# Three slices of the first expert layer's weights on chip, their loads moved, its units taken in threes

## The chip, the cores and the metric

One NeuronCore of a Trainium2 chip runs the whole program; the other cores idle. The metric is the device time of one launch in microseconds (us), as the median of several runs. TensorE (PE) multiplies matrices, VectorE (DVE), ScalarE (ACT) and GpSimd (POOL) work elementwise, SyncE (SP) only issues transfers; each engine takes its instructions strictly in its own order. ACT issues transfers too.

## The reference

Three stages, on 4 batches of 576 tokens (2304 rows of 512 after attention).

```
a = softmax of phi over the sequence;  k_m = a.T @ k;  v_m = a.T @ v      # 32 memory slots a head
x = softmax(q @ k_m.T / 8) @ v_m                                          # 8 heads of 64, joined to 512
h = x @ w_in;  x = (h * cos(h)) @ w_out                                   # w_in 512x2048, w_out 2048x512
out = sum over 4 experts e of p[:, e] * (relu(x @ w1[e]) @ w2[e])         # p = domain_probs, rows scaled to sum 1
```

## The kernel before

**Numbers.** A float32 operand of a large product is split into a rounded high part and the rest, both of type fp32r, and a product is three matmuls (`mm3`, L145): high by high, high by low, low by high. `w_in` and `w_out` arrive as 64-bit floats: `narrow` (L122) loads a chunk of 512 KB into one of two buffers `raw64`, ACT rescales it (L131), and DVE shifts and merges the halves in three passes (L132, L133, L136) into 32-bit floats. `split_w` (L106) then makes the two parts of a `w_out` slice, with ACT (L109) and four pieces on POOL, or two on POOL and two on DVE for slices after the second (L111).

**Attention** is a generator (L167) of 8 parts, two groups of four heads for each batch. A part loads phi, then k, v and q; takes a maximum (DVE L189), an exponential (ACT L207) and a sum (L209) over the sequence; projects k and v on the 32 slots (PE L221); and makes scores (PE L271), which DVE transposes (L278) and reduces (L281), POOL subtracts (L282), ACT exponentiates (L285), DVE sums and inverts (L286 to L288), POOL scales (L289) and DVE transposes back (L293); ACT and POOL split the result into `attnT` (L103, L104). k and v share three buffers `kv`, phi and q have two each.

**The first expert layer** is cut into 8 slices of 256 hidden columns. A unit is a slice and a batch: `project` (L316) folds v into the slice of `w_in` (PE, 16 records of `vw_ps`); `hidden1` (L333) makes h on PE (24 matmuls of `hp`) and h times cosine on ACT, DVE (L360, L365, L104) and POOL; `output1` (L369) multiplies with `w_out` (48 matmuls of `op`), and DVE adds the results into `acc` (L384 for slice 0, L386 after it). While attention still runs, units are in a narrow form (one chunk of 128 hidden columns at a time, POOL subtracts, DVE makes the low part of `gt`); afterwards in a wide form (L354), which takes both chunks in one instruction.

**Order of the units.** `order` (L391) runs slices 0 and 1 over all batches first (8 units), and then slices 2 to 7, each over the four batches. Buffers: `wi` and `wo` two each, `wf` one. Slice 0's `w_in` is issued by SP ahead of the loads of batch 1, and its `w_out` and all of slice 1 by ACT, each behind one of the first exponentials (`exps`). Six units stand among the attention parts 2 to 7, one to a part, each behind its part's scores (L438 to L441); the seventh and later ones are wide. Slice 2 is loaded from units 6 and 8 on, and later slices during the slice ahead of them (L402).

**What sets the order.** The program is traced in the order of the code, and a scheduler then lays it out engine by engine along a time line of its own, so that an instruction may move far from its place in the code. SP's queue is strictly in order too: a transfer that waits for a buffer holds up those behind it.

**The second expert layer** (L459 on) follows; its code is the same in both kernels. The sums of `domain_probs` that it needs (`load_probs`, L92) are loaded by POOL near the start: 2304 pieces of 16 bytes.

Of the kernel before, what the change touches and what calls it, by code (L numbers as in the profile page):

```python
# [9 lines left out]
F32 = mybir.dt.float32  # L10
F32R = mybir.dt.float32r
# [13 lines left out]
def tile_kernel(  # L25
# [13 lines left out]
    nc = tc.nc  # L39
    B, H, S, D = q.shape  # L40
    M = phi.shape[3]
    NT, DM = out.shape
# [6 lines left out]
    KD = DM // 128  # L49
    FS = 256  # L50
    NFC = FS // 128
    NS1 = DFF // FS
# [37 lines left out]
    p_all = const.tile([128, NT // 128, E], F32, name="p_all")  # L90

    def load_probs():  # L92
        nc.gpsimd.dma_start(out=p_all, in_=probs.rearrange("(i p) e -> p i e", p=128))
        p_sum = const.tile([128, NT // 128], F32, name="p_sum")
        nc.vector.tensor_reduce(out=p_sum, in_=p_all, axis=AX.X, op=ALU.add)
        nc.vector.tensor_scalar_add(p_sum, p_sum, 1e-9)
        nc.vector.reciprocal(out=p_sum, in_=p_sum)
        nc.vector.tensor_tensor(
            out=p_all, in0=p_all, in1=p_sum[:, :, None].to_broadcast([128, NT // 128, E]), op=ALU.mult
        )  # L100

    def split(hi, lo, src, eng=None):
        nc.scalar.activation(out=hi, in_=src, func=ACTF.Copy)  # L103
        (eng or nc.vector).tensor_tensor(out=lo, in0=src, in1=f32(hi), op=ALU.subtract)  # L104

    def split_w(t, src, early=False):  # L106
        t, src = t.rearrange("p x a b -> p x (a b)"), src.rearrange("p a b -> p (a b)")
        n = src.shape[1]
        nc.scalar.activation(out=t[:, 0], in_=src, func=ACTF.Copy)  # L109
        for c in range(0, n, 256):  # L110
            (nc.vector if early and c % 512 else nc.gpsimd).tensor_tensor(  # L111
                out=t[:, 1, c:c + 256], in0=src[:, c:c + 256], in1=f32(t[:, 0, c:c + 256]), op=ALU.subtract
            )
# [8 lines left out]
    def narrow(w, src, after=None, part=None):  # L122
        n, m = w.shape[1:]
        c = 1024 // (2 * m)
        for i in range(0, n, c) if part is None else (part * c,):
            raw = cw.tile([128, c, 2 * m], U32, tag="raw64", name="raw64")
            with tc.issue_after(after.ins) if after else nullcontext():
                (nc.scalar if after else nc.sync).dma_start(out=raw, in_=src[:, i:i + c])
            lo, hi = (raw.rearrange("p a (b t) -> p a b t", t=2)[:, :, :, t] for t in range(2))
            hif = raw.bitcast(F32).rearrange("p a (b t) -> p a b t", t=2)[:, :, :, 1]  # L130
            nc.scalar.activation(out=hif, in_=hif, func=ACTF.Copy, scale=2.0 ** -112)  # L131
            nc.vector.tensor_single_scalar(lo, lo, 29, op=ALU.logical_shift_right)  # L132
            nc.vector.scalar_tensor_tensor(  # L133
                out=lo, in0=hi, scalar=3, in1=lo, op0=ALU.logical_shift_left, op1=ALU.bitwise_or
            )
            nc.vector.scalar_tensor_tensor(  # L136
                out=w[:, i:i + c].bitcast(U32),
                in0=hi,
                scalar=0x80000000,
                in1=lo,  # L140
                op0=ALU.bitwise_and,
                op1=ALU.bitwise_or,
            )
# [13 lines left out]
    cw = cs_ctx.enter_context(tc.tile_pool(name="cw", bufs=2))  # L157
    mb = cs_ctx.enter_context(tc.tile_pool(name="mb", bufs=1))
    cs = cs_ctx.enter_context(tc.tile_pool(name="cs", bufs=2))
# [5 lines left out]
    exps = []  # L165
# [133 lines left out]
    wi = {}  # L299
    wo = {}  # L300
    wf = [None]

    def load_in(s, after=None, part=None):
        if not part:
            wi[s] = cw.tile([128, KD, FS], F32, tag="wi", name="wi")
        narrow(wi[s], w_in_v[:, :, 2 * s * FS:2 * (s + 1) * FS], after, part)

    def load_out(s, after=None, part=None):
        if not part:
            wf[0] = cw.tile([128, NFC, DM], F32, tag="wf", name="wf", bufs=1)  # L310
        narrow(wf[0], w_out_v[:, s * NFC:(s + 1) * NFC, :], after, part)
        if part != 0:
            wo[s] = cs.tile([128, 2, NFC, DM], F32R, tag="wo", name="wo")
            split_w(wo[s], wf[0], s > 1)

    def project(b, wi):  # L316
        vw_ps = ps_o.tile([128, 2, FS], F32, tag="o", name="vw_ps")
        for g in range(2):
            for i in range(HG):
                nc.tensor.matmul(  # L320
                    out=vw_ps[32 * i:32 * i + 32, g, :],
                    lhsT=vz[b][:, g, i, :],
                    rhs=wi[:, 2 * g + i // 2, :],
                    start=True,
                    stop=True,
                )
        vw = cs.tile([128, 2, 2, FS], F32R, tag="vw", name="vw")
        split(vw[:, 0], vw[:, 1], vw_ps)
        return vw
# [39 lines left out]
    def output1(s, b, th, gt, wo):  # L369
        for d in range(KD):  # L370
            c = d % 2 if wide[0] else 0
            op = (ps_o, ps_a)[c].tile([128, 512], F32, tag="oa"[c], name="op")
            for fc in range(NFC):
                mm3(
                    op[:, :TH],
                    lambda x: wo[:, x, fc, d * 128:d * 128 + 128],
                    lambda x: gt[:, x, fc, :],
                    fc == 0,
                    fc == NFC - 1,
                )  # L380
            t0 = (b % 2) * S
            dst = x1v[:, b // 2, d, t0:t0 + S].rearrange("p (c u) -> p u c", u=2)[:, th]
            if s == 0:
                nc.vector.tensor_copy(out=dst, in_=op[:, :TH])  # L384
            else:
                nc.vector.tensor_tensor(out=dst, in0=op[:, :TH], in1=dst, op=ALU.add)  # L386
# [1 line left out]
    vws = {}  # L388
    wide = [False]
    pend = []  # L390
    order = [(s, b) for b in range(B) for s in range(2)]  # L391
    order += [(s, b) for s in range(2, NS1) for b in range(B)]

    def project_next(n):
        if n + 1 < len(order):
            s2, b2 = order[n + 1]
            vws[n + 1] = project(b2, wi[s2])

    def step1(n):
        s, b = order[n]  # L400
        for th in range(2):
            if n > 8 and b in (1, 2) and s + 1 < NS1:  # L402
                (load_in, load_out)[b - 1](s + 1, marks[-1], th)
            pend.append((s, b, th, hidden1(b, th, vws[n]), wo[s]))
            if len(pend) > 2:
                output1(*pend.pop(0))
            if th == 0:
                project_next(n)

    parts = [attention(b, g) for b in range(B) for g in range(2)]  # L410
# [3 lines left out]
    def warm_up(n):  # L414
        for _ in range(n):
            nc.tensor.matmul(out=warm, lhsT=ones, rhs=ones, start=True, stop=True)

    for i in (0, 1, 0, 1, 0, 1, 0, 0, 1, 1):
        next(parts[i], None)
    warm_up(25)  # L420
    load_in(0)
    load_out(0, exps[0])
    vws[0] = project(0, wi[0])
    for i in (2, 2, 3, 2, 3):
        next(parts[i])
    load_in(1, exps[0])
    load_out(1, exps[1])
    nu = 0
    for n in range(2, np_):
        part = parts[n]  # L430
        if n + 2 < np_:
            next(parts[n + 2])
        if n + 1 < np_:
            next(parts[n + 1])
        if n + 2 < np_:
            next(parts[n + 2])
        next(part)
        next(part, None)  # L438
        if n <= 7:
            step1(nu)  # L440
            nu += 1  # L441
    wide[0] = True
    c_ctx.close()
    ps_h[0] = p_ctx.enter_context(tc.tile_pool(name="ps_h2", bufs=2, space=PSUM, reuse_waits="tile"))
    load_probs()
    at_ctx.close()
    wc = ctx.enter_context(tc.tile_pool(name="wc", bufs=2, side="right", reuse_waits="tile"))
    for n in range(nu, len(order)):
        s, b = order[n]
        if n == 6:  # L450
            load_in(2)
        if n == 8:
            load_out(2)
        step1(n)
    for p in pend:
        output1(*p)
# [216 lines left out]
```

## Time and profile before

| | |
|---|---|
| median of 3 runs | 1220.98 us (1220.67 to 1222.85) |
| profiled execution | 1223.36 us, its span 1221.6 us |
| PE busy | 1181.9 us, 97% of the span |
| DVE, ACT, POOL busy | 868.2, 485.6, 525.2 us |
| moved by transfers | 72.89 MB |

The page splits the span into 40 slices of 30.5 us and gives in each the busy share of every engine, the clock granted to TensorE and the transfers. PE is short of full in the first five slices alone. Attention fills about the first 160 us; from there to 440 us the first expert layer runs alone, and then the second to the end.

### The profile page before, as it was taken

What the parts mean: (1) busy time and instruction counts of PE and PEld (TensorE: products, weight loads), DVE (VectorE), ACT (ScalarE), POOL (GpSimd) and SP (SyncE); (2) the same over time, 40 slices, a digit from 0 to 9 for tenths busy, and PEclk for the clock granted to TensorE, in tenths of its full rate; (3) what the DMA queues carried; (4) which work ended last, traced back from release to release, by engine and by line L of the source; (5) the groups of instructions that cost most, each with busy time, mean ns of one, the idle gap of its engine ahead of it and who ended that gap; (6) DMA issues with size and microseconds to landing.
All of it is one profiled execution on the core that took longest, in us unless ns stands there. A gap on an engine that the chain in (4) does not pass through costs nothing.

```text
span 1221.6 us, 20025 instructions
## 1 busy us (share of the span) xinstructions
PE 1181.9 (97%) x7946; PEld 1050.3 (86%) x7946; DVE 868.2 (71%) x1571; ACT 485.6 (40%) x854; POOL 525.2 (43%) x609
## 2 busy tenths in 40 slices
PE   6788999999999999999999999999999999999998
PEld 5466788999999988888889898898889989888997
DVE  5798988798788788666666666678656665666665
ACT  2475755666566663232222223244222322322221
POOL 1443533332333852445445445546534544453420
PEclk8589999999999999999999999999999999999999
DMA  9953001112112110111111111113111111111102
GB/s 224 251 147 77 21 36 52 36 53 70 35 36 72 52 52 18 37 52 51 35 53 53 35 40 57 43 36 129 54 35 50 55 35 35 53 52 36 52 1 78
DMA packets 48062, 72.89 MB, mean 60 GB/s; under 512 B 2624, under 2 KB 31328, under 8 KB 47968
## 3 DMA queue, kind: packets, MB, share of 16 engines
q1 hardware_dynamic: 41024, 55.85, 16.1%
q10 hardware_dynamic: 6880, 15.73, 4.2%
q8 instruction: 62, 1.02, 0.3%
q14 instruction: 32, 0.26, 0.1%
q0 software_dynamic: 64, 0.04, 0.0%
HBM read 66.88 MB, written 4.72 MB: 59 GB/s over the span
## 4 chain that ended last, share of the span: by engine, by line
PE 62%; DVE 1%; issue 0%
PE op L147 33%; PE hp L147 29%; DVE x L485 1%; DVE sA L477 0%; DVE sB L498 0%; DVE acc L617 0%; DVE ht L582 0%; DVE u L558 0%; DVE acc L386 0%
## 5 line engine op out<-in xcount | busy, mean ns | idle before, releaser
L147 PE MATMUL op<-wb,ht 128*128 128x512 f32 x1728 | 439.3, 396 | 0.0
L147 PEld LDWEIGHTS hp<-x,wa 128*128 128x128 f32 x2688 | 380.3, 189 | 24.4 <-DVE x L485 3.6
L147 PE MATMUL hp<-x,wa 128*128 128x320 f32 (+1 forms) x2688 | 393.6, 295 | 3.2 <-DVE x L485 2.9
L147 PEld LDWEIGHTS op<-wb,ht 128*128 128x128 f32 x1728 | 312.7, 188 | 58.5
L617 DVE SCALAR_TENSOR_TENSOR acc<-op,p_all,acc 128x512 f32<-128x512 f32 x270 | 201.8, 748 | 137.7 <-PE op L147 137.4
L147 PE MATMUL op<-gt,wo 128*128 128x288 f32 x1536 | 228.8, 298 | 6.3 <-DVE acc L384 3.2
L147 PEld LDWEIGHTS op<-gt,wo 128*128 128x128 f32 x1536 | 211.7, 189 | 13.1 <-DVE acc L384 4.0
L111 POOL TENSOR_TENSOR wb<-raw,wb 128x256 fp32r<-128x256 f32 x124 | 89.5, 753 | 227.2 <-ACT wb L109 227.2
L588 ACT ACTIVATE ht<-c 128x256 fp32r<-128x256 f32 (+3 forms) x128 | 71.8, 562 | 283.5 <-DVE c L558 283.5
L104 POOL TENSOR_TENSOR gt<-y,gt 128x576 fp32r<-128x576 f32 x52 | 81.4, 1566 | 163.2 <-ACT gt L103 138.5
L589 DVE SCALAR_TENSOR_TENSOR ht<-c,ht 128x256 fp32r<-128x256 f32 (+3 forms) x128 | 93.7, 732 | 63.1 <-ACT ht L588 63.1
L147 PE MATMUL hp<-attnT,vw 128*128 128x288 f32 x768 | 129.6, 304 | 4.9 <-DVE y L365 3.8
L528 POOL TENSOR_TENSOR wa<-raw,wa 128x256 fp32r<-128x256 f32 x96 | 69.2, 748 | 149.1 <-ACT wa L518 149.1
L147 PEld LDWEIGHTS hp<-attnT,vw 128*128 128x128 f32 x768 | 109.6, 190 | 19.1 <-issue 14.3
L558 DVE TENSOR_TENSOR c<-hp,u 128x256 f32<-128x256 f32 (+1 forms) x192 | 87.3, 457 | 42.3 <-PE hp L147 37.9
L528 POOL TENSOR_TENSOR wa<-tt,wa 128x256 fp32r<-128x256 f32 x128 | 110.0, 889 | 0.0
L386 DVE TENSOR_TENSOR acc<-op,acc 128x288 f32<-128x288 f32 x224 | 96.5, 450 | 16.5 <-PE op L147 16.1
L565 ACT COPY p<-hp 128x256 f32<-128x256 f32 x64 | 25.7, 401 | 113.0 <-PE hp L147 113.0
L364 ACT ACTIVATE y<-y 128x576 f32<-128x576 f32 (+1 forms) x76 | 46.1, 609 | 61.3 <-DVE y L356 52.9
L103 ACT ACTIVATE gt<-y 128x576 fp32r<-128x576 f32 (+1 forms) x76 | 46.0, 605 | 37.6 <-DVE y L365 37.5
L518 ACT ACTIVATE wa<-raw 128x512 fp32r<-128x512 f32 x32 | 20.2, 632 | 85.5 <-PE hp L147 85.3
L365 DVE TENSOR_TENSOR y<-hp,y 128x576 f32<-128x576 f32 (+1 forms) x76 | 49.7, 655 | 5.2 <-ACT y L364 5.0
(101 smaller groups left out, 1062.4 us busy)
## 6 DMA issues: line engine op xcount, KB each, us to landing
raw<-in_moe_w_dram SPq DMA_DIRECT2D x60, 512.0 KB, 3.5
raw<-in_moe_w_out_dram ACTq DMA_DIRECT2D x14, 512.0 KB, 3.5
raw<-in_moe_w_in_dram ACTq DMA_DIRECT2D x12, 512.0 KB, 3.7
kv<-in_k_dram SPq DMA_DIRECT2D x16, 288.0 KB, 6.2
kv<-in_v_dram SPq DMA_DIRECT2D x16, 288.0 KB, 7.1
q<-in_q_dram SPq DMA_DIRECT2D x8, 576.0 KB, 9.2
out_dram<-acc SPq DMA_DIRECT2D x18, 256.0 KB, 2.0
phi<-in_phi_dram SPq DMA_DIRECT2D x8, 288.0 KB, 7.9
```

What stands on the lines that cost most here:

```text
L103: nc.scalar.activation(out=hi, in_=src, func=ACTF.Copy)
L104: (eng or nc.vector).tensor_tensor(out=lo, in0=src, in1=f32(hi), op=ALU.subtract)
L111: (nc.vector if early and c % 512 else nc.gpsimd).tensor_tensor(out=t[:, 1, c:c + 256], in0=src[:, c:c + 256], in1=f32(t[:, 0, c:c + 256]) ...
L147: nc.tensor.matmul(out=ps, lhsT=lt(a), rhs=rt(b), start=first and i == 0, stop=last and i == 2, skip_group_check=more,)
L364: nc.scalar.activation(out=y, in_=y, func=ACTF.Sin, scale=-TWO_PI if wide[0] else TWO_PI)
L365: nc.vector.tensor_tensor(out=y, in0=hv, in1=y, op=ALU.mult)
L386: nc.vector.tensor_tensor(out=dst, in0=op[:, :TH], in1=dst, op=ALU.add)
L528: pool.tensor_tensor(out=wa[:, 1, o], in0=src, in1=f32(wa[:, 0, o]), op=ALU.subtract)
L558: nc.vector.tensor_tensor(out=out, in0=ps[:, :n], in1=sb, op=ALU.add)
L588: nc.scalar.activation(out=ht[:, 0, fc, lo:], in_=c[:, fc, lo:], func=ACTF.Relu)
L589: nc.vector.scalar_tensor_tensor(out=ht[:, 1, fc, lo:], in0=c[:, fc, lo:], scalar=0.0, in1=f32(ht[:, 0, fc, lo:]), op0=ALU.max, op1=ALU.su ...
L617: nc.vector.scalar_tensor_tensor(out=dst, in0=op, scalar=pe, in1=dst, op0=ALU.mult, op1=ALU.add)
```

## The change

Three slices are on chip at first instead of two (`bufs=3` for `wi` and `wo`), and the order of units becomes slices 0, 1 and 2 over all batches (12 units), then 3 to 7. All weight loads at the start are issued by SP: slice 0 right behind the loads of batch 0, slice 1's `w_in` ahead of the second pair of attention parts and its `w_out` behind their loads, slice 2 at part 2. The first unit is traced ahead of part 2's scores, and after that one unit follows an even part and two an odd one, so that nine narrow units are traced among the parts instead of six. `domain_probs` is loaded by SP. The memory kept for POOL's own transfers is cut to 2048 bytes.

```diff
-        nc.gpsimd.dma_start(out=p_all, in_=probs.rearrange("(i p) e -> p i e", p=128))
+        nc.sync.dma_start(out=p_all, in_=probs.rearrange("(i p) e -> p i e", p=128))
...
-            wi[s] = cw.tile([128, KD, FS], F32, tag="wi", name="wi")
+            wi[s] = cw.tile([128, KD, FS], F32, tag="wi", name="wi", bufs=3)
...
-            wo[s] = cs.tile([128, 2, NFC, DM], F32R, tag="wo", name="wo")
+            wo[s] = cs.tile([128, 2, NFC, DM], F32R, tag="wo", name="wo", bufs=3)
...
-    order = [(s, b) for b in range(B) for s in range(2)]
-    order += [(s, b) for s in range(2, NS1) for b in range(B)]
+    NE = 3
+    order = [(s, b) for b in range(B) for s in range(NE)]
+    order += [(s, b) for s in range(NE, NS1) for b in range(B)]
...
-            if n > 8 and b in (1, 2) and s + 1 < NS1:
+            if n >= NE * B and b in (1, 2) and s + 1 < NS1:
...
-    for i in (0, 1, 0, 1, 0, 1, 0, 0, 1, 1):
+    for i in (0, 1, 0, 1):
+        next(parts[i], None)
+    load_in(0)
+    load_out(0)
+    for i in (0, 1, 0, 0, 1, 1):
         next(parts[i], None)
     warm_up(25)
-    load_in(0)
-    load_out(0, exps[0])
     vws[0] = project(0, wi[0])
+    load_in(1)
     for i in (2, 2, 3, 2, 3):
         next(parts[i])
-    load_in(1, exps[0])
-    load_out(1, exps[1])
+    load_out(1)
...
+        if n == 2:
+            step1(nu)
+            nu += 1
+            load_in(2)
+            load_out(2)
         next(part)
         next(part, None)
-        if n <= 7:
+        for _ in range(n % 2 if n == 2 else 1 + n % 2):
             step1(nu)
             nu += 1
...
-        if n == 6:
-            load_in(2)
-        if n == 8:
-            load_out(2)
+        if n == NE * B - 3:
+            load_in(NE)
+        if n == NE * B - 1:
+            load_out(NE)
...
-    nc = _bacc.Bacc("TRN2", target_bir_lowering=False, num_devices=1)
+    nc = _bacc.Bacc("TRN2", target_bir_lowering=False, num_devices=1, dynamic_dma_scratch_size=2048)
```

The queue of SP before, from the second half of slice 0's `w_in` on (`kv_128` is the last of the k and v of part 1, `kv_426` the first of part 2):

```order
L128 DMA raw64_387<-in_moe_w_in_dram 128x2x512
L171 DMA phi_424<-in_phi_dram 96x4x192
L182 DMA q_432<-in_q_dram 96x4x384
L178 DMA kv_128<-in_k_dram 96x2x384
L179 DMA kv_128<-in_v_dram 96x2x384
L178 DMA kv_426<-in_k_dram 96x2x384
L179 DMA kv_426<-in_v_dram 96x2x384
L171 DMA phi_434<-in_phi_dram 96x4x192
```

The same place of SP's queue in the changed kernel:

```order
L128 DMA raw64_140<-in_moe_w_in_dram 128x2x512
L93 DMA p_all_91<-in_moe2_domain_probs_dram 128x18x4
L171 DMA phi_437<-in_phi_dram 96x4x192
L182 DMA q_445<-in_q_dram 96x4x384
L171 DMA phi_447<-in_phi_dram 96x4x192
L178 DMA kv_128<-in_k_dram 96x2x384
L179 DMA kv_128<-in_v_dram 96x2x384
L178 DMA kv_439<-in_k_dram 96x2x384
L179 DMA kv_439<-in_v_dram 96x2x384
```

The scheduler put the `domain_probs` of a part of the program 400 us later, and the phi of part 3, ahead of `kv_128`, which part 1 waits for.

DVE before, around the transposes (L278) of part 4's scores `st_1033`:

```order
L278 STREAM_TRANSPOSE st_1033<-sc_1037 128x288
L365 TENSOR_TENSOR y_885<-hp_902,y_885 128x288
L278 STREAM_TRANSPOSE st_1033<-sc_1043 128x288
L293 STREAM_TRANSPOSE stT_787<-st_784 128x576
L386 TENSOR_TENSOR acc_73<-op_1106,acc_73 128x288
L104 TENSOR_TENSOR gt_887<-y_885,gt_887 128x288
L201 TENSOR_TENSOR a_1211<-phi_948,bcs_1209 96x4x6x32
```

DVE in the changed kernel, around the transposes of the same part's scores, `st_1203` there (`wo_662` is slice 2, `raw64_2348` and `raw64_2354` are slice 3's `w_in`):

```order
L111 TENSOR_TENSOR wo_662<-wf_649,wo_662 128x256 x2
L195 TENSOR_SCALAR dg_1375<-ident_74,mxT_1373 128x128
L360 TENSOR_SCALAR kk_918<-y_917 128x288
L384 COPY acc_73<-op_964 128x288
L278 STREAM_TRANSPOSE st_1203<-sc_1207 128x288
L132 TENSOR_SCALAR raw64_2354<-raw64_2354 128x512
L278 STREAM_TRANSPOSE st_1203<-sc_1213 128x288
L133 SCALAR_TENSOR_TENSOR raw64_2348<-raw64_2348 128x512
L365 TENSOR_TENSOR y_917<-hp_920,y_917 128x288
L384 COPY acc_73<-op_972 128x288
L293 STREAM_TRANSPOSE stT_819<-st_816 128x576
L201 TENSOR_TENSOR a_1381<-phi_1118,bcs_1379 96x4x6x32
```

Before, no weights pass DVE here; now the passes of slice 2's `w_out` and slice 3's `w_in` stand between the attention instructions.

## Rows read from the trace of the kernel before

**Rows 1.** The page, busy tenths and granted clock in 40 slices

```profile
PE   6788999999999999999999999999999999999998
DVE  5798988798788788666666666678656665666665
PEclk8589999999999999999999999999999999999999
```

**Rows 2.** Windows, all engines: stretch, length, busy us and instructions, clock, transfers

```profile
20.00:40.00 20.00, 13.18 (x132) 7.80 (x126) 15.18 (x37) 7.32 (x16) 5.30 (x7) 0.74 1.10 262
40.00:60.00 20.00, 12.70 (x102) 9.07 (x105) 17.20 (x33) 11.05 (x24) 9.84 (x10) 0.57 1.01 237
60.00:160.00 100.00, 89.59 (x831) 70.12 (x824) 90.07 (x194) 67.84 (x128) 45.75 (x43) 0.93 0.31 79
200.00:440.00 240.00, 239.34 (x1952) 222.00 (x1952) 198.78 (x364) 149.31 (x234) 101.92 (x84) 1.00 0.18 56
```

**Rows 3.** Timeline of DVE: start, length, line, operation, [idle before it]

```profile
53.69 0.27 DVE L288 RECIPROCAL ssm<-ssm 128x9 f32<-128x9 f32 x2
...
98.17 1.44 DVE L189 TENSOR_REDUCE mx<-phi 96x128 f32<-96x768 f32 x1 [1.97 <-DMA phi<-in_phi_dram]
...
109.82 1.56 DVE L209 TENSOR_REDUCE asum<-a 96x128 f32<-96x768 f32 x1 [3.98 <-ACT qT L215]
...
158.32 0.77 DVE L293 STREAM_TRANSPOSE stT<-st 128x576 f32<-128x576 f32 x1
```

**Rows 4.** Timeline of PE: loads, a first unit, part 7's scores, a projection

```profile
29.72 2.78 PE L221 MATMUL kvp<-kv,a 96*32 96x128 f32 x44 [1.93 <-DMA kv<-in_v_dram]
...
57.54 1.98 PE L147 MATMUL hp<-attnT,vw 128*128 128x288 f32 x6
...
146.55 1.18 PE L271 MATMUL sc<-qT,kz 128*32 128x288 f32 x16
...
431.93 1.07 PE L320 MATMUL vw_ps<-wi,vz 128*32 128x256 f32 x16
```

**Rows 5.** Windows, PE alone: transfers and the microseconds around POOL's load of `domain_probs`

```profile
7.00:8.00 1.00, 1.00 (x11) 1.00 1.18 90
8.00:9.00 1.00, 0.95 (x9) 1.00 0.94 154
9.00:10.00 1.00, 0.00 (x0) 1.00 1.07 238
```

**Rows 6.** Transfer queues of SP (q1, 0 to 12 us) and ACT (q10, 12 to 40)

```profile
q1 hardware_dynamic: 1853, 2.11, 87.8%
...
q10 hardware_dynamic: 288, 1.05, 12.6%
```

**Rows 7.** DVE by line and shape, 0 to 165 us: count, busy us, mean ns

```profile
L104 DVE TENSOR_TENSOR gt<-y,gt 128x288 fp32r<-128x288 f32 x22 | 12.7, 582 | 0.0
L360 DVE TENSOR_SCALAR kk<-y 128x288 f32<-128x288 f32 x24 | 11.9, 501 | 0.6 <-ACT y L353 0.6
L365 DVE TENSOR_TENSOR y<-hp,y 128x288 f32<-128x288 f32 x23 | 10.2, 442 | 1.9 <-ACT y L364 1.9
L384 DVE COPY acc<-op 128x288 f32<-128x288 f32 x21 | 9.2, 448 | 0.2
L133 DVE SCALAR_TENSOR_TENSOR raw<-raw 128x512 uint32<-128x512 uint32 x10 | 7.2, 722 | 0.0
L132 DVE TENSOR_SCALAR raw<-raw 128x512 uint32<-128x512 uint32 x10 | 5.4, 540 | 2.5 <-DMA raw<-in_moe_w_in_dram 2.5
L136 DVE SCALAR_TENSOR_TENSOR wi<-raw 128x512 uint32<-128x512 uint32 x6 | 5.0, 839 | 0.0
```

**Rows 8.** DVE by line and shape, 165 to 420 us

```profile
L111 DVE TENSOR_TENSOR wo<-wf,wo 128x256 fp32r<-128x256 f32 x12 | 7.8, 693 | 0.6 <-ACT wo L109 0.4
```

**Rows 9.** Windows, PE alone: narrow units without scores, and wide units

```profile
147.50:165.00 17.50, 16.23 (x135) 1.00 0.03 10
280.00:380.00 100.00, 100.00 (x824) 1.00 0.18 54
```

## The prediction, written before the changed kernel had run

> **What bounds the kernel now.** First the slices of the page [rows 1]: PE is full from the sixth slice to the end, and the clock is at its upper level there; what it lacks, it lacks in the first 150 us. So the change is worth what it does to that stretch, and every microsecond by which PE's work stands later at its end reaches the end of the kernel. Then the windows [rows 2]: from 20 to 60 us PE is busy 13 of 20 us, at a granted clock of 0.74 and 0.57 (a mixture of 1.2 and 2.4 GHz), and the transfers run at 237 to 262 GB/s, with every transfer engine busy. From 60 to 160 us PE is busy 89.6 of 100 us, DVE 90.1, POOL 46, and the transfers are three tenths busy. From 200 to 440 us PE is full and DVE busy 199 of 240. So the start is bound by the loads, the attention stretch by DVE, and the rest by PE. The timelines show the bound changing hands [rows 3, 4]: part 1 waits for its last v until 29.7 us; its reciprocals stand on DVE until 53.7 us behind rows for the next parts and for weights; the first unit can use part 1's result at 57.5; the last part's scores run on PE at 146.6 and its result is transposed back on DVE at 158.3.
>
> From 60 us on a part of attention costs DVE more than PE and a unit costs PE more than DVE. Whatever else is put on DVE before 158 us therefore comes out of the units that PE could have been fed.
>
> **The change part by part.** The orders of the two kernels, compared up to the transpose back of the last part (158.32 us before), agree in everything of attention. The rest differs.
>
> Start of the units. In SP's queue `kv_128`, part 1's last k and v, now has part 3's phi ahead of it: 295 KB at 257 GB/s at most, 1.1 us (rates between 237 and 262 in [rows 2]). It also has `domain_probs` ahead of it. That load, issued by POOL before, held the transfers down to 90 and 154 GB/s in two microseconds, against 238 right after [rows 5]: 148 + 84 KB lost, 1.0 us. This is given back, since the early bytes now move without it. What the same 2304 pieces cost in SP's queue no row shows. Lower bound: as much as before, 1.0 us. Upper bound: a packet for each piece. SP's packets of 1.1 KB took 0.878 x 12 us x 16 engines / 1853 = 91 ns, ACT's of 3.6 KB 0.126 x 28 x 16 / 288 = 196 ns [rows 6]; a line through the two leaves some 43 ns for a packet without bytes, and 2304 x 43 ns / 16 = 6.2 us. I take 1.5, near the row of the same pieces. So `kv_128` lands 1.1 - 1.0 + 1.5 = 1.6 us later, with bounds of 1.1 and 6.3. On DVE the reciprocals of part 1 stand two rows earlier than before (ahead of part 3's `a` and the next maximum, 1.1 + 1.4 us), yet still behind the first chunk of slice 1, which SP now issues behind the k and v of parts 2 and 3, and the POOL rows that scale the result stand behind four pieces of slice 0's `w_out`, as before. These about cancel: the first unit starts **1.5 us** later (from 1 us earlier, if the two rows gain all of their time, to 6 later).
>
> DVE rows. Ahead of the last transpose back there are now four more each of L132 and L133 (slice 2's `w_out` and slice 3's `w_in`) and of L136 (slice 2, whose `w_in` waited for its buffer until after that point before): 4 x (0.540 + 0.722 + 0.839) = 8.4 us [rows 7]. And two pieces of slice 2's split, 2 x 0.693 = 1.4 us [rows 8]. Units have fewer rows ahead of that point: one L104, one L365, two L360 and five L384, together 4.3 us [rows 7]. Net 5.5 us, less 0.07 us of overlap for each of five more rows (in the timeline a row starts about that much before the one ahead ends): **+5.2 us** for the last part. Bounds: 0, if they fall into DVE's idle time (9.9 us of the 100), and 8.7, if the rows taken out were not what DVE was busy with.
>
> PE's place at that point. Ahead of the last part's scores PE had 114 `hp` and 168 `op` matmuls behind it; in the changed order it has 102 and 144. So 36 matmuls, that stood beside attention, are left for later, when PE is full. A unit has 88 records at 100 us / 824 = 121 ns [rows 9], 10.7 us, of which 1.07 is the projection [rows 4]; 72 matmuls in 9.6 us are 0.133 each, and 36 are **+4.8 us** (nothing, if PE does them in gaps). The name of the change speaks of more units beside attention; by the order fewer are done when it ends, since the units wait for DVE.
>
> Three more narrow units. Between the last scores and the wide form PE takes 17.5 us / 135 = 129.6 ns a record, afterwards 121.4 [rows 9]. 3 units x 88 x 8.2 ns = **+2.2 us**; between nothing and this, since the stretch has some of the last softmax in it; I keep it, since DVE's own rows of a narrow unit stay.
>
> Stalls. DVE's longest waits from 60 us on were for a phi that came behind a q (1.97) and, in its wake, for an exponential (3.98) [rows 3]. In the new queue that phi stands ahead of the q. Against that, `raw64` has two buffers, and SP now takes the chunks of slice 2 in line with k and v, so that a late pass of DVE holds up loads of a part. **-3 us**, between -6 and +3.
>
> Nothing from 200 us on: the last units and all of the second layer stand in the same order on every engine. The third buffers of `wi` and `wo` cost memory and no time.
>
> Sum: 1.5 + 5.2 + 4.8 + 2.2 - 3.0 = +10.7 us. Against the profiled execution of 1223.36 us this is 1234.1; that execution lies 2.4 us above the median of the runs, 1220.98, and I predict from the median: 1231.7 us.
>
> The Trainium skill, page DMA: Bandwidth & Descriptors, section Specifications, says that transfers under 512 B lose the line rate, since the engine reads, modifies and writes. The row of POOL's load agrees that small pieces take more than their bytes [rows 5]: 37 KB cost 232 KB. If each of the 2304 pieces cost as much as 512 B, it would be an estimate of 1.18 MB at 238 GB/s, 5.0 us instead of 1.5, and the sum +14.2. Neither end of my range rests on it.
>
> **The rivals.** One: idle time, not work, holds DVE up. With a third slice on chip there is always another unit's row to put between two that depend on each other, and the waits close. DVE idles 4.8, 2.8 and 9.9 us in the three stretches [rows 2], 17.5 together; the terms above without the stalls cost 13.7. From 13.7 us closed on the change is faster; if all is closed, 3.8 us: 1217.2. For it: the idle time is there, and much of it is in waits of one engine for another. Against it: the stretch to 60 us idles for loads, which a unit doesn't bring sooner, and after part 3 the two orders hold nearly the same rows. Two: `domain_probs` goes out piece by piece and holds the loads of batches 0 and 1 by the upper bound, 6.2 instead of 1.5 us: +15.4, 1236.4. For it: the pieces are as small, and `kv_128` stands right behind. Against it: the same pieces cost 1.0 us in POOL's queue. Three: no change. DVE's rows fall into its idle time (0 for 5.2), the full 6 us of the two stalls go and the start isn't later: 4.8 + 2.2 - 6 = +1.0, 1222.0. For it: DVE is at 90%, not 100. Against it: between waits it runs row on row.
>
> **How the numbers follow.** My forecast 0.58, the idle time 0.20, the slow pieces 0.12, no change 0.10. The forecast's own range, with the start and the stalls at their ends, is 1226 to 1242. The range that should hold the time 8 times in 10 runs from 1216, a little beyond the full closing of the idle time, to 1242, beyond the slow pieces. A measurement of this kernel tells about 0.2% (2.4 us) from no change. Slower by more: the forecast and the slow pieces, 0.70; within: 0.10; faster: 0.20.
>
> **What would show it.** Right: the last transpose back (L293 of 128x576) comes near 164 us instead of 158.3, with about 36 fewer `hp` and `op` records ahead of the last scores; DVE busy in 60 to 160 us stays at 90 or more, with 14 rows each of L132 and L133 by then instead of 10. Start: a wait of PE for a k or v near 31 us. Narrow: about 130 ns a record until some 200 us. Wrong: DVE idle well under 10 us in that stretch and PE full before 140 us (the idle time was it); a run of some 6 us with transfers far under 200 GB/s between 22 and 32 us (the slow pieces). If the last part is transposed before 158 us, the whole account of DVE falls.

## The result: slower by 1.0%, and the profile after

| | before | after |
|---|---|---|
| median, us (lowest to highest) | 1220.83 (1220.17 to 1222.85) | 1232.93 (1231.65 to 1234.00) |
| ratio, 95% interval | | 1.0100 [1.0082, 1.0119] |
| profiled execution, its span, us | 1223.36, 1221.6 | 1233.57, 1231.8 |
| DVE's last transpose back, start | 158.32 | 163.20 |

The page's slices of the changed kernel, busy tenths and granted clock, stand against [rows 1]:

```profile
PE   7868999999999999999999999999999999999998
DVE  5798887787788888666656656678665665665665
PEclk7577999999999999999999999999999999999999
```

From the fifth slice on nothing in these three rows differs but tenths of DVE; the clock is lower in the first, third and fourth (7, 7 and 7 against 8, 8 and 9). The windows of the changed kernel, all engines (stretch, length, busy us and instructions of PE, PEld, DVE, ACT and POOL, clock, share of the transfer engines, GB/s), against [rows 2]:

```profile
20.00:40.00 20.00, 14.89 (x121) 8.84 (x121) 16.45 (x42) 6.41 (x14) 5.09 (x7) 0.50 1.04 252
40.00:60.00 20.00, 16.70 (x118) 10.80 (x118) 16.31 (x32) 10.11 (x20) 10.18 (x10) 0.50 0.87 222
60.00:160.00 100.00, 84.17 (x748) 65.82 (x746) 90.17 (x188) 67.49 (x123) 43.81 (x41) 0.84 0.38 99
200.00:440.00 240.00, 238.95 (x1952) 221.89 (x1951) 193.89 (x363) 145.54 (x231) 93.02 (x78) 1.00 0.16 50
```

From 60 to 160 us DVE is as busy as before, 90.17 against 90.07 us, and PE has 83 instructions fewer. From 200 to 440 us PE has the same 1952. The loss is made ahead of 200 us and never given back: counted along PE's timeline, its 1150th instruction starts 10.3 us later than before (168.1 against 157.8 us), its 2000th 10.1 us later. Where it sits can be narrowed: PE alone, from 60 to 120 us, first before, then after (busy us and instructions, clock, transfers):

```profile
60.00:120.00 60.00, 52.09 (x485) 0.89 0.48 121
```

```profile
60.00:120.00 60.00, 46.36 (x384) 0.74 0.60 155
```

A hundred matmuls are missing there. DVE's timeline of the changed kernel (start, length, line, operation, [idle before it]) shows what it did instead; it answers to [rows 3]:

```profile
56.59 0.77 DVE L195 TENSOR_SCALAR dg<-ident,mxT 128x128 f32<-128x128 f32 x1
60.93 0.43 DVE L132 TENSOR_SCALAR raw<-raw 128x512 uint32<-128x512 uint32 x1 [3.57 <-DMA raw<-in_moe_w_out_dram]
61.27 0.68 DVE L104 TENSOR_TENSOR vw<-vw_ps,vw 128x512 fp32r<-128x512 f32 x1
...
86.45 0.81 DVE L384 COPY acc<-op 128x288 f32<-128x288 f32 x2
...
115.68 0.46 DVE L386 TENSOR_TENSOR acc<-op,acc 128x288 f32<-128x288 f32 x1 [3.26 <-PE op L147]
...
163.20 0.76 DVE L293 STREAM_TRANSPOSE stT<-st 128x576 f32<-128x576 f32 x1
```

At 57.4 us a weight pass stood at the head of DVE's queue, its chunk (slice 1's `w_out`) still under way, with the first unit's rows behind it: 3.6 us. The first result of a unit is taken off PE at 86.45 us; in the kernel before this row is

```profile
73.61 0.80 DVE L384 COPY acc<-op 128x288 f32<-128x288 f32 x2
```

12.8 us earlier. Yet the first unit's matmuls on part 1's result began earlier after the change, at 55.45 us against 57.54, as PE's timeline shows against [rows 4]:

```profile
29.64 2.78 PE L221 MATMUL kvp<-kv,a 96*32 96x128 f32 x44 [1.59 <-DMA kv<-in_v_dram]
...
55.45 0.85 PE L147 MATMUL hp<-attnT,vw 128*128 128x288 f32 x2 [0.16 <-ACT attnT L103]
```

And DVE's passes by line, 0 to 165 us (count, busy us, mean ns, idle before), against [rows 7] and [rows 8]:

```profile
L133 DVE SCALAR_TENSOR_TENSOR raw<-raw 128x512 uint32<-128x512 uint32 x14 | 10.1, 720 | 0.0
L132 DVE TENSOR_SCALAR raw<-raw 128x512 uint32<-128x512 uint32 x14 | 6.2, 445 | 3.8 <-DMA raw<-in_moe_w_out_dram 3.6 <-DMA raw<-in_moe_w_in_dram 0.2
L136 DVE SCALAR_TENSOR_TENSOR wf<-raw 128x512 uint32<-128x512 uint32 x6 | 5.0, 830 | 0.0
L136 DVE SCALAR_TENSOR_TENSOR wi<-raw 128x512 uint32<-128x512 uint32 x6 | 4.7, 777 | 0.0
L111 DVE TENSOR_TENSOR wo<-wf,wo 128x256 fp32r<-128x256 f32 x2 | 2.0, 1036 | 0.0
```

The whole in one row each, 0 to 160 us, first before, then after:

```profile
0.00:160.00 160.00, 128.90 (x1166) 99.24 (x1167) 131.51 (x285) 90.38 (x174) 62.98 (x66) 0.85 0.58 137
```

```profile
0.00:160.00 160.00, 131.27 (x1104) 99.28 (x1104) 131.60 (x279) 90.29 (x168) 59.79 (x63) 0.75 0.60 150
```

DVE worked the same 131.5 us. PE ran 62 instructions fewer, and was longer at them, with the lower clock.

### The profile page after: what moved, and what is told of

It is laid out like the page before. It is cut to its first block, busy times and chain, and to the rows that moved or that the text cites. A ratio compares the mean times of both kernels' runs of the same rounds, so it can differ in the third digit from the quotient of the medians.

```text
span 1231.8 us, 20085 instructions
## 1 busy us (share of the span) xinstructions
PE 1192.6 (97%) x7946; PEld 1058.4 (86%) x7946; DVE 874.6 (71%) x1595; ACT 486.2 (39%) x866; POOL 523.7 (43%) x614
## 4 chain that ended last, share of the span: by engine, by line
PE 85%; DVE 9%; DMA 3%; ACT 2%; issue 1%; SPq 0%; POOL 0%; DVEq 0%; ACTq 0%; POOLq 0%
PE op L147 46%; PE hp L147 35%; PE vw_ps L320 2%; DMA raw<-in_moe_w_out_dram 1%; DVE gt L104 1%; PE kvp L221 1%; DVE acc L386 1%; DMA q<-in_q_dram 1%; DVE x L493 1%; DVE kk L360 1%; DMA kv<-in_v_dram 1%; DVE y L365 1%; DMA phi<-in_phi_dram 0%; PE pq L214 0%; DVE acc L384 0%
## 5 line engine op out<-in xcount | busy, mean ns | idle before, releaser
L111 POOL TENSOR_TENSOR wb<-raw,wb 128x256 fp32r<-128x256 f32 x124 | 89.5, 753 | 224.7 <-ACT wb L109 224.7
L147 PE MATMUL hp<-attnT,vw 128*128 128x288 f32 x768 | 132.1, 307 | 4.8 <-DVE y L365 3.1
L104 POOL TENSOR_TENSOR gt<-y,gt 128x576 fp32r<-128x576 f32 x46 | 72.1, 1567 | 147.0 <-ACT gt L103 118.2
L147 PEld LDWEIGHTS hp<-attnT,vw 128*128 128x128 f32 x768 | 112.5, 194 | 17.0 <-issue 10.0
L386 DVE TENSOR_TENSOR acc<-op,acc 128x288 f32<-128x288 f32 x224 | 96.9, 450 | 20.9 <-PE op L147 20.6
L364 ACT ACTIVATE y<-y 128x576 f32<-128x576 f32 (+1 forms) x82 | 47.2, 578 | 55.7 <-DVE y L356 41.9
L363 POOL TENSOR_TENSOR y<-y,kk 128x288 f32<-128x288 f32 x36 | 31.2, 867 | 57.3 <-DVE kk L360 53.3
```

The source lines that it names most:

```text
L147: nc.tensor.matmul(out=ps, lhsT=lt(a), rhs=rt(b), start=first and i == 0, stop=last and i == 2, skip_group_check=more,)
L363: nc.gpsimd.tensor_tensor(out=y, in0=y, in1=kk, op=ALU.subtract)
L364: nc.scalar.activation(out=y, in_=y, func=ACTF.Sin, scale=-TWO_PI if wide[0] else TWO_PI)
```

## The experiments

Twelve kernels, each timed against the kernel before. To compare them I split DVE's time up to the end of its last transpose back (T) by what its rows are for, from each kernel's timeline; a row counts until the next one begins, and in brackets stands how many rows start ahead of the last transpose back. (The four rows of `domain_probs`, 0.8 us, are in no column; writing constants at the start, 1.2 us, is in the idle time.) The rest of the span behind T is the work that PE has left. These numbers are worked out from many rows, so no view shows them; x9, whose program runs the same instructions as the kernel before, tells how far single terms scatter (up to 3 us). Passes are the rows on weights (L132, L133, L136 and the split L111), units those of the first expert layer.

```
us         T    attention  passes (rows)  units (rows)  idle   rest    span   ratio to before, 95% interval
before   159.1    67.9      17.2 (28)     43.6 (103)    29.7  1062.5  1221.6
after    164.0    68.5      24.9 (42)     40.1 (94)     29.6  1067.8  1231.8  1.0100 [1.0082, 1.0119]
x1       168.7    68.1      23.9 (42)     45.0 (106)    31.7  1061.5  1230.2  1.0107 [1.0086, 1.0128]
x2       166.1    69.0      24.0 (38)     43.0 (100)    29.3  1062.8  1229.0  1.0073 [1.0052, 1.0095]
x3       164.5    68.3      25.2 (42)     41.2 (94)     28.9  1067.3  1231.8  1.0092 [1.0073, 1.0112]
x4       166.0    69.1      24.0 (38)     41.3 (102)    30.9  1068.9  1234.9  1.0139 [1.0118, 1.0161]
x5       175.3    69.8      18.2 (30)     50.9 (120)    35.6  1054.8  1230.1  1.0079 [1.0062, 1.0096]
x6       175.9    67.5      26.5 (42)     49.3 (109)    31.8  1059.6  1235.5  1.0123 [1.0103, 1.0142]
x7       177.6    68.2      17.6 (30)     51.8 (117)    39.2  1055.4  1233.0  1.0090 [1.0072, 1.0108]
x8       177.5    67.7      24.3 (38)     50.4 (117)    34.3  1055.3  1232.8  1.0098 [1.0074, 1.0121]
x9       160.5    65.6      16.5 (28)     45.0 (103)    32.6  1060.2  1220.7  1.0004 [0.9993, 1.0014]
x10      167.9    68.2      23.5 (36)     45.0 (103)    30.4  1062.7  1230.6  1.0080 [1.0063, 1.0096]
x11      163.5    66.3      19.5 (28)     40.2 (94)     36.7  1060.7  1224.2  1.0045 [1.0031, 1.0059]
x12      174.4    67.9      28.8 (42)     41.6 (98)     35.4  1060.6  1235.0  1.0118 [1.0100, 1.0135]
```

What the table says: more unit rows ahead of T move T and take about as much off the rest (x5: +7.3 and -7.7; x7: +8.2 and -7.1; x8: +6.8 and -7.2; in x6 only half, +5.7 and -2.9). Passes and idle time are not given back. Their two differences with the kernel before come to most of the span's in many kernels: after 7.6 of 10.2, x1 8.7 of 8.6, x2 6.4 of 7.4, x3 7.2 of 10.2, x5 6.9 of 8.5, x6 11.4 of 13.9, x7 9.9 of 11.4, x8 11.7 of 11.2, x10 7.0 of 9.0. They don't in the others: x4 8.0 of 13.3 (it loses time behind T), x11 9.3 of 2.6 and x12 17.3 of 13.4 (part of the unit rows is on another engine), and x9 2.2 of -0.9, where there is nothing to explain. So the split is a way of adding up, and within some 2 to 3 us it proves nothing.

My theory was the prediction's: passes and less unit work beside attention. The first rivals were `domain_probs` in SP's queue, the early part (loads, DVE's 3.6 us, clock) and idle time that takes the passes.

**x1: `domain_probs` late, off SP's queue.** In `load_probs` of the changed kernel:

```
-        nc.sync.dma_start(out=p_all, ...)
+        with tc.issue_after(marks[-1].ins):
+            nc.scalar.dma_start(out=p_all, ...)
```

> The changed kernel, with domain_probs loaded by ACT's queue behind the first units instead of at the head of SP's queue. In the order the weight passes of DVE ahead of the last transpose back stay (14, 14 and 12), and PE has 18 hp, 30 op and 8 vw_ps matmuls more behind it at the last scores (120, 174 and 48). By the account of DVE rows and PE's place: the extra unit rows on DVE put the last transpose back some 5 us later than 163.2, the 56 matmuls are worth 56 x 0.133 = 7.4 us, and the transfers win about 1.3 us at the start: 1232.9 - 3.7 = 1229 us, ratio to the kernel before 1.007. If the 2304 pieces in SP's queue were the cause: 1232.9 - 6 = 1227 or less, with the first unit's hp 5 us earlier than 55.45. If neither matters: 1233.

No gain: 1234.92 us. The load is not the cause. The clock is not needed either. Here it was 0.86 up to T, as high as before, and the profiled span is still 8.6 us above that of the kernel before (10.2 in the changed kernel):

```profile
0.00:168.70 168.70, 129.02 (x1176) 99.85 (x1180) 138.21 (x296) 93.42 (x180) 62.50 (x67) 0.86 0.58 143
```

**x2: two slices, the early part kept.**

```
-    NE = 3
+    NE = 2
...
-            load_in(2)
-            load_out(2)
...
-        for _ in range(n % 2 if n == 2 else 1 + n % 2):
+        for _ in range(n > 2):
```

(and the conditions on `n` for the loads of slice 2 as before.)

> The changed kernel with two slices through the attention instead of three: one unit behind each part as before the change, slice 2 loaded where the kernel before loads it; the early loads, the first unit ahead of part 2's scores and domain_probs on SP's queue stay. By the order 12, 12 and 12 weight passes on DVE ahead of the last transpose back instead of 14, 14, 12, and 24 hp and op matmuls more behind PE at the last scores. By the account: DVE -2.5 for the passes, +2.9 for unit rows, PE's place -24 x 0.133 = -3.2, three narrow units fewer -2.2: 1232.9 - 5.0 = 1227.9 us, ratio 1.006. If the early part of the change (queue, first unit, clock from 20 to 60 us) were the cause of the loss, it stays above 1231; if the third slice is the whole cause, 1221.

1229.96 us, some 3 us below the changed kernel, as the account had it but for 2 us. Most of the loss stays without the third slice. But the third buffers were still there, and through them 38 pass rows.

**x3: one unit behind each part.** The last line of the diff of x2 alone.

> The changed kernel with one unit written behind each part instead of one and two: the order is the same on DVE and PE up to the last scores, and only the units behind them take the wide form three units sooner. By the account -2.2 us: 1230.7 us, ratio 1.008. If the narrow form costs nothing here: 1232.9, ratio 1.010. More than 4 us would show that the narrow units after attention cost more than their own records on PE.

1233.59 us: no gain. Its interval leaves room for 2 us, and the profiles show where a gain can have gone. From 160 to 170 us x3 ran at a lower clock and 10 matmuls fewer; from 180 to 210 us, where its units were wide and those of the changed kernel still narrow (the first wide row on DVE starts at 181 and at 216 us), it ran 10 more. First after, then x3:

```profile
160.00:170.00 10.00, 8.54 (x60) 1.00 0.01 2
180.00:210.00 30.00, 28.64 (x232) 1.00 0.04 9
```

```profile
160.00:170.00 10.00, 8.44 (x50) 0.83 0.00 1
180.00:210.00 30.00, 29.30 (x242) 1.00 0.00 2
```

Ten matmuls at 0.12 us are 1.2 us: about so much the narrow form costs there, and the median doesn't show it.

**x4: slice 3's `w_in` held back.**

```
-            load_in(NE)
+            load_in(NE, marks[-1])
```

> The changed kernel with slice 3's w_in issued by ACT only behind a unit's first activation, so that its passes on DVE (two of the four chunks' L132 and L133) stand behind the last transpose back; PE has 12 hp and 18 op matmuls more behind it at the last scores. By the account: DVE's passes -2.5, unit rows in their place +3.8, PE's place -30 x 0.133 = -4.0: 1232.9 - 2.7 = 1230.2 us, ratio 1.0075. If DVE's idle time took the passes: 1232.9. If the clock of 20 to 120 us is the cause of the loss: 1232.9 and the same clocks there.

1237.99 us, slower still. Up to T passes fell only from 24.9 to 24.0. PE, full in the changed kernel from 300 to 400 us, now lost 2 us there; PE alone, first after, then x4:

```profile
0.00:200.00 200.00, 169.05 (x1401) 0.80 0.48 121
300.00:400.00 100.00, 100.00 (x824) 1.00 0.19 58
```

```profile
0.00:200.00 200.00, 163.22 (x1414) 0.85 0.47 115
300.00:400.00 100.00, 98.04 (x792) 1.00 0.17 52
```

By 200 us x4 had run 13 matmuls more than the changed kernel, some 1.6 us of PE's work. So up to there it had gained, as the account had it (2.7 us expected), though by no more than x9 scatters. It lost more than that later, and not for want of the held slice: its last pass starts at 212 us, its first unit's projection at 238 us. Why it lost there stays open.

**x5: two of three passes left out from slice 2 on.** The changed kernel; the weights of these slices are not the right ones.

```
+            if not short:
                 nc.vector.tensor_single_scalar(lo, lo, 29, ...)
                 nc.vector.scalar_tensor_tensor(out=lo, in0=hi, scalar=3, in1=lo, ...)
...
-                in1=lo,
+                in1=hi if short else lo,
```

> The changed kernel with the first two of the three DVE passes of a weight chunk (L132 and L133) left out for the slices from 2 on, so that those weights are not the right ones; every load, wait and buffer stays. Ahead of the last transpose back stand 8 L132 and 8 L133 instead of 14, about 7 us of DVE less, and by the order unit rows take their place: 30 hp, 60 op and 8 vw_ps matmuls more behind PE at the last scores. If passes on DVE displace unit rows: the last transpose back moves +12.7 - 7.0 us, PE's place is worth 98 x 0.133 = 13.0, together 1232.9 - 7.3 = 1225.6 us, ratio 1.004. If the early part (the loads in SP's queue, DVE's 3.57 us at slice 1's w_out chunk, the clock from 20 to 60 us) is the cause: 1231 or more.

1231.76 us: of 7.3 us expected, 1.2 came by the medians and 2.6 by the ratios, whose intervals overlap. Passes went down by 6.7 us and the unit rows went up, as the order had it; but T moved to 175.3 and DVE's idle time rose by 6.0. My account, which charges rows and no waits, fails here.

**x6: the loads back on ACT's queue.** The changed kernel, its start written as before:

```
-    for i in (0, 1, 0, 1):
+    for i in (0, 1, 0, 1, 0, 1, 0, 0, 1, 1):
...
+    load_in(0)
+    load_out(0, exps[0])
...
+    load_in(1, exps[0])
+    load_out(1, exps[1])
```

> The changed kernel with the weight loads of slices 0 and 1 written where and issued as in the kernel before (slice 0's w_out and all of slice 1 on ACT's queue behind the exponentials of part 0); three slices, third buffers and domain_probs in SP's queue stay. By the account of passes alone: passes as in the changed kernel, unit rows +7.2 us, PE's place 56 x 0.133 = 7.4 us: no gain, 1232.7 us, ratio 1.010. If the early part is the cause: the first result of an op on DVE comes at about 74 us instead of 86.5 and the time is near 1224, ratio 1.003.

1236.84 us. The first result came at 73.2 us, 13 us earlier, as the rival had it, and the kernel is no faster. So the late first result, which looks like the cause in the timeline, is not what costs.

**x7: the early part alone.** The kernel before with the diff's lines on the start, `domain_probs` and the scratch size, two slices, two buffers, and

```
+        if n == 2:
+            step1(nu)
+            nu += 1
...
-        if n <= 7:
+        for _ in range(n > 2):
```

> The kernel before with the early part of the change alone: weight loads of slices 0 and 1 in SP's queue at the changed places, domain_probs in SP's queue, the first unit ahead of part 2's scores; two slices with two buffers each, one unit behind each part. Ahead of the last transpose back 10, 10 and 10 passes (before 10, 10, 8). By the account of passes: unit rows and L136 +8.6 us, PE's place 62 x 0.133 = 8.2: +0.4, 1221.9 us, ratio 1.000. If the early part is the cause: +8 us or more, 1229.5, ratio 1.007.

1232.73 us: it alone loses as much as the whole change, with hardly a pass more. It is idle time: +9.5 us. DVE's waits around the last softmaxes (in total, times, longest), first of the kernel before from 120 to 160 us, then of x7 from 120 to 178 us:

```profile
DVE y L365 <- ACT y L364: 1.9, 3, 0.9
DVE kk L360 <- ACT y L353: 0.6, 2, 0.4
DVE acc L386 <- PE op L147: 0.2, 1, 0.2
```

```profile
DVE ssm L286 <- ACT st L285: 3.9, 3, 1.8
DVE y L365 <- ACT y L364: 3.8, 4, 1.4
DVE kz L251 <- PE pkt L247: 1.2, 1, 1.2
DVE acc L384 <- PE op L147: 1.1, 4, 0.4
```

DVE takes its rows in order, and here it stands at rows whose exponential or sine ACT hasn't finished. What ACT did before them is seen in its timeline: a load of a function table, 1.28 us in every such row, between the exponentials (L207, L285) and the sines (L364). Two of the waits, on DVE and then on ACT:

```profile
133.38 0.75 DVE L286 TENSOR_REDUCE ssm<-st 128x18 f32<-128x576 f32 x1 [1.76 <-ACT st L285]
...
136.16 0.46 DVE L365 TENSOR_TENSOR y<-hp,y 128x288 f32<-128x288 f32 x1 [1.43 <-ACT y L364]
```

```profile
131.37 1.28 ACT L285 ACT_TABLE_LOAD   x1
132.66 0.68 ACT L285 ACTIVATE st<-st 128x576 f32<-128x576 f32 x1
133.25 0.39 ACT L353 ACTIVATE y<-hp 128x288 f32<-128x288 f32 x1
133.54 0.83 ACT L207 ACTIVATE a<-a 96x768 f32<-96x768 f32 x1
134.40 1.28 ACT L364 ACT_TABLE_LOAD   x1
135.69 0.44 ACT L364 ACTIVATE y<-y 128x288 f32<-128x288 f32 x1
```

Counted over both timelines up to T, 8 waits of x7, 10.1 us, end with an activation right behind such a load; before it is 4 waits and 2.2 us (in x9 5 waits and 3.5 us), though both kernels have 14 loads there. So x7 has no more of them, but its order hides fewer. No run here takes the loads away, so how much of the 9.5 us they cost is not shown.

**x8: third buffers alone.** The kernel before, with the scratch size at 4096 to make room:

```
-            wi[s] = cw.tile([128, KD, FS], F32, tag="wi", name="wi")
+            wi[s] = cw.tile([128, KD, FS], F32, tag="wi", name="wi", bufs=3)
...
-            wo[s] = cs.tile([128, 2, NFC, DM], F32R, tag="wo", name="wo")
+            wo[s] = cs.tile([128, 2, NFC, DM], F32R, tag="wo", name="wo", bufs=3)
```

> The kernel before with the third buffers of wi and wo alone. They let slice 2's loads, and with them 2 L132, 2 L133, 4 L136 and 2 L111 more on DVE, go ahead of the last transpose back; by the order 18 hp, 36 op and 8 vw_ps matmuls more stand there too. By the account of passes: DVE +6.9 for passes and +7.0 for unit rows, PE's place 62 x 0.133 = 8.2: +5.7, 1227.2 us, ratio 1.005. If a third buffer costs no time, as the prediction says: 1221.5, ratio 1.000.

1235.11 us, 9 to 15 us slower by the interval. My sentence that they cost no time is wrong: they let slice 2's chunks go ahead of T, 7.1 us of passes more, and idle time rose by 4.6. The two prices do not add up: x2 is x7 with the third buffers, and loses 1.0073 [1.0052, 1.0095], no more than either alone.

**x9: the scratch size alone.** The kernel before:

```
-    nc = _bacc.Bacc("TRN2", target_bir_lowering=False, num_devices=1)
+    nc = _bacc.Bacc("TRN2", target_bir_lowering=False, num_devices=1, dynamic_dma_scratch_size=4096)
```

x8 sets it to this, the changed kernel and x1 to x7 to 2048, so it had to be told apart.

> The kernel before with dynamic_dma_scratch_size=4096 and nothing else (the changed kernel sets 2048, x8 set 4096); the order of instructions is that of the kernel before on every engine. All kernels tried so far set it and all are 8 to 15 us slower, so it has to be told apart. If the scratch size, or where it puts the tiles, is the cause: 1229 us or more. By every account of DVE: no change, 1221.5 us, ratio 1.000.

1.0004 [0.9993, 1.0014]: nothing. (2048 was not tried alone; x10 and x11 leave the size as it was and lose time too.) It gives a second profile of the same instructions. Clock and idle time differ from the first one's (0.85; 128.90 and 131.51 us of PE and DVE in 160), the time doesn't:

```profile
0.00:160.00 160.00, 132.45 (x1156) 100.83 (x1157) 128.53 (x282) 89.67 (x171) 61.66 (x66) 0.83 0.58 137
```

**x10: passes alone.** The kernel before; for slices 0 and 1:

```
+            for _ in range(2 if twice else 1):
                 nc.vector.scalar_tensor_tensor(out=w[:, i:i + c].bitcast(U32), ...)
```

> The kernel before with the third pass of a weight chunk (L136) done twice for slices 0 and 1, so 8 passes more on DVE ahead of the last transpose back and not a byte more of loads; hp matmuls ahead of the last scores as before, 6 op and 8 vw_ps more. By the account of the time up to the last transpose back (its attention rows 68 us in every kernel, then passes, unit rows and idle time; a microsecond of unit rows is given back later, a microsecond of passes or idle time is not): 8 x 0.84 = +6.7 us, 1228.5 us, ratio 1.0055. If passes fall into DVE's idle time, as they seemed to in x5: 1222, ratio 1.000.

1231.40 us, +9.8 by the ratio (7.7 to 11.7 by the interval). Eight rows of DVE, 6.3 us more of passes in the profile, cost more than their own time: DVE's idle time took none of them (30.4 against 29.7). The rival, "idle time takes them", falls. But the order moved too: ACT has 16 table loads up to T instead of 14 (so have x6, x11 and x12), so it is not passes alone on every engine.

**x11 and x12: unit rows from DVE to POOL.** In the kernel before and in the changed one:

```
-            split(..., y, nc.gpsimd if wide[0] else nc.vector)
+            split(..., y, nc.gpsimd if wide[0] or f0 % 2 else nc.vector)
```

> The kernel before with every second split of a narrow unit (L104, gt) on POOL instead of DVE: 11 rows of 0.58 us, 6.4 us, leave DVE ahead of the last transpose back, with the rest of the order nearly as before. By the account of DVE's time: the last transpose back some 6 us earlier and the kernel faster than both, 1216 us, ratio 0.9955; if POOL's slower split (about 1.0 us) ends in DVE's or PE's waits instead, no change or slower, 1221 to 1226.

> The changed kernel with every second split of a narrow unit (L104, gt) on POOL instead of DVE: 8 rows fewer of L104 on DVE ahead of the last transpose back, against 2 L360, 2 L365, 3 L384 and 4 L386 more by the order; 18 hp, 30 op and 8 vw_ps matmuls more behind PE at the last scores. By the account of DVE's time: passes stay, the unit rows taken out are 8 x 0.58 = 4.6 us, so 1232.9 - 4.6 = 1228.3 us, ratio 1.006. If DVE's waits for other engines set the time there: 1233 or more, as in x5 and x7, with DVE's idle time up by what its rows went down.

1226.47 and 1236.49 us. x11 is slower than the kernel before; x12's median is above the changed kernel's, but the intervals overlap. In x11 unit rows fell by 3.4 us and idle time rose by 7.0: DVE again waits for sines, 6.6 us from 55 to 180 us (2.1 before). A split took POOL 933 ns, against 582 on DVE [rows 7]. So DVE's rows bind in one direction: adding some costs, taking some away to a slower engine is no gain. No kernel tried is faster than the kernel before.

## Why the prediction was right, and where it wasn't

1231.7 us was predicted and 1232.93 measured; 10.7 us by the sum, 12.1 by the medians, 10.2 by the two profiles.

- **DVE rows, +5.2.** Right as seen: the last transpose back is 4.9 us later, 14 rows each of L132 and L133, and DVE's idle time did not take them (29.7 and 29.6). By the split, passes +7.7 (forecast 8.4 + 1.4), unit rows -3.5 (forecast -4.3). x10 shows that 6.3 us of passes can cost this much and more.
- **PE's place +4.8 and narrow units +2.2.** Together 7.0, measured as the rest behind T: +5.3. PE's place is there: in the stretch up to T, first before, then after, PE runs 1159 and 1124 instructions, 35 fewer, against 36 by the order. Of the narrow term x3's profile shows about 1.2, and its median nothing.

```profile
0.00:159.05 159.05, 127.95 (x1159) 98.29 (x1160) 130.56 (x283) 89.43 (x172) 62.98 (x66) 0.85 0.58 138
```

```profile
0.00:163.96 163.96, 134.18 (x1124) 101.96 (x1125) 135.53 (x288) 92.39 (x173) 61.71 (x65) 0.76 0.59 147
```

- **Start, +1.5.** Wrong in sign. PE's wait for v was as before, `domain_probs` cost little, and the first unit could use part 1's result 2.1 us earlier; what I took for the start, these matmuls, was the wrong mark, since the unit's first result is 12.8 us late. x6 shows that this mark decides nothing either.
- **Stalls, -3.** Nothing came. The two waits of [rows 3] went, and new ones of 3.57, 3.26, 1.35 and 1.30 us took their place. The first is a chunk that stood behind k and v in SP's queue; the risk that I had named was the reverse, a part's loads behind a chunk. I had also misread the wait of 3.98 us before: its row names the copy of `qT` (L215), and ACT had finished the exponential 2.3 us ahead of DVE's start at 109.82 us:

```profile
106.65 0.84 ACT L207 ACTIVATE a<-a 96x768 f32<-96x768 f32 x1
...
109.22 0.54 ACT L215 COPY qT<-pq 128x288 f32<-128x288 f32 x1
```

- **Clock.** Not foreseen: 0.50 from 20 to 60 us. x1 and x10 lose 8.6 and 9.0 us of span at 0.86 and 0.83 up to T. Whether it adds to the loss of the changed kernel I did not try.
- **Rivals.** Idle time that closes: it did not. No change: 10 to 14.5 us by the interval exclude it. Slow pieces: x1 excludes them. In SP's queue `domain_probs` went out as 2304 packets of 16 bytes from 18.6 to 20.9 us; their own times add up to 21.0 us, 1.3 us on 16 engines, near the 1.5 that I took: 9 ns each, and not the 43 of the upper bound. One microsecond shows it, 46 GB/s at full engines. That 1.5 was near is luck, since it came from POOL's load, which the profile page of the kernel before has as 64 packets and not as the same pieces. The Trainium skill (DMA: Bandwidth & Descriptors, Specifications) says that transfers under 512 B lose the line rate. The trace agrees (46 GB/s), but not with the 5.0 us that the prediction estimated by it. First the two microseconds, then the row of POOL's queue before (packets, MB, share):

```profile
18.00:19.00 1.00, 1.00 (x12) 0.50 1.11 318
19.00:20.00 1.00, 1.00 (x6) 0.50 1.05 46
```

```profile
q0 software_dynamic: 64, 0.04, 0.0%
```

So the mechanism was right in kind, DVE rows and PE's place together (forecast 10.0; T moved by 4.9 us, and the rest behind it, narrow units included, by 5.3). That the sum came so near is in part luck: +1.5 and -3.0 were wrong and +2.2 was about half, and the three together came to only +0.7. What the prediction lacked is shown by x5, x7 and x8: parts of this change do not add up. By the medians the early part alone costs 10 us, the third buffers alone 13, both together 8 (x2), the whole 12. In x5 and x7, which have fewer passes, idle time of DVE comes in their place, at rows that stand at the head of its queue too early; in x7 most of the rise is in waits that end behind ACT's table loads (10.1 against 2.2 us). Why the order of the kernel before hides them best, and which single row of a new order lays them bare, stays open; the order alone did not let me foresee it (x5 and x7 were both expected 6 to 11 us faster than they are).

## What to carry to other kernels

Where one engine takes rows of two chains in order and is busy nine tenths, split its time up to the end of the stretch into the chain that must end, work that is only early, and idle time: early work that the rest would have hidden is a loss, early work that the rest needs is neutral. Charge waits as well as rows, and look at what the releasing engine did just before it released. Test parts of a change alone, and don't add up their prices. A late milestone in a timeline is not a cause until moving it moves the end (x6).

## What the runs showed that I had not expected

Two profiles of the same instructions (before and x9) differ by 0.83 and 0.85 in mean granted clock over 160 us and by 3.6 us in PE's busy time, and the kernel's time is the same: in this stretch PE, longer at the same work at the lower of its two clock levels, seems to have used time in which it would have waited. The mean of a weight pass scatters between kernels by more than the edits explain: L133 took 722 ns before, 693 in x9 with the same instructions, 804 in x10, and 781 and 870 in x11 and x12, where POOL has half of the unit splits. Since x10 is as long with no split on POOL, POOL is not shown to be the cause.
